# Attention scores from four half-height products a head, two heads side by side in 128 rows

## The chip, the cores and the metric

One Trainium2 chip, one core of it. The metric is the time of one execution in device microseconds; several runs are made and their median is taken. TensorE (PE) multiplies, VectorE (DVE) and ScalarE (ACT) work elementwise, GpSimd (POOL) does the same more slowly and issues some DMAs, SyncE (SP) issues most DMAs.

## The reference

Attention with a learned decay over 4 batches, 8 heads, 576 positions and 64 columns, then two mixture layers on the 2304 tokens. The change is in the attention alone:

```python
scores = scale * np.matmul(q, k.transpose(0, 1, 3, 2))
cum = np.cumsum(np.log(np.clip(f, 0.0001, 1.0)), axis=-1)
decay = cum[:, :, :, None] - cum[:, :, None, :]
scores = np.where(causal, -1000000000.0, scores + decay)
scores = scores - np.max(scores, axis=-1, keepdims=True)
attn = np.exp(scores)
attn = attn / (np.sum(attn, axis=-1, keepdims=True) + 1e-09)
return np.matmul(attn, v).astype(np.float32)
...
x = _moe_ref(x=x, **moe_kwargs)       # leaky relu between two matrices
return _moe2_ref(x=x, **moe2_kwargs)  # eight experts of fixed capacity
```

## The kernel before

The program has stages behind one another: attention (with the first products of the first mixture layer mixed in), the rest of that layer, the choice of experts, the experts. The change lies in the first, which ends with the last product av at 290.8 us of the profile.

Attention goes over 16 pairs of heads (`heads`), and each pair through three functions. `prepare` loads q and k, transposes them on TensorE into tile T, with both heads in 128 rows, and splits each number into a high part in float32r and the rest, the low part. `offsets` multiplies queries by keys with the queries in rows, finds each row's maximum on VectorE (into `nm`, tile `kept` holds the masked scores), sums the exponentials on ScalarE (into `sm`) and sends the maxima as rows back into the operands. `attend` makes the scores again, keys in rows, takes the exponential on ScalarE (P<-st), cuts at the diagonal on GpSimd, multiplies by v (av) and scales.

A score needs high x high, low x high, high x low and the added rows (running sum of the decay, maximum). Before, one head's operands fill the height of the array: `qa` has high over low parts, `ka` the high part twice, so qa x ka is one product of 128 rows; `qb` has the high part again and below it ones and maxima, `kb` the low part, running sums and ones, so qb x kb is the second, of 96 rows in `offsets` and of 128 in `attend` (lines 697, 698, 805 and 806). The second copies, in `ka`'s lower and `qb`'s upper half, are made by a DMA inside SBUF in every pair but the first (lines 643 and 645), and the first has extra ScalarE instructions instead (`again`, line 630). High and low parts are made a head at a time, in 64 rows (lines 602 to 615).

A block is a rectangle of queries and keys that are not all cut off: in `offsets` 64 and 192, 320, 448 and twice 288 keys for 128 queries, in `attend` 320, 448, 320 and 192, 256 and 64 queries for 128 keys. Each product goes into one PSUM bank of 128 x 512: tag `mx` with two banks for `offsets`, `st` with two for `attend`, one head at a time; T has two, av and h one each.

The order of work is set by `Plan.order`: each step is an `op` with an engine, an assumed duration, needs, a rank (12 a pair, plus places within it) and the buffers it takes and uses; a list scheduler lays the steps out, and they are issued in that order on each engine (`InOrder`). `mm_ns` (line 502) is the assumed duration of products: columns over 2.4 GHz, at least 107 ns, plus 3, a product; it has no term for a change between shapes of the array. All these steps have line 62 in the profile, so groups are told apart by tile. The early products h<-X,wh (line 904) and the preparation of weights (w, wbits, wsq, wst, wh) have ranks of their own and fill in.

av multiplies two heads in the two halves of the columns (64 each); T's last piece of each q and k has 64 rows.

Of the kernel before, what the change touches and what calls it, by code (L numbers as in the profile page):

```python
# [12 lines left out]
FT = mybir.dt.float32  # L13
FR = mybir.dt.float32r
# [3 lines left out]
OP = mybir.AluOpType  # L18
# [27 lines left out]
NK = 4  # L46
TB = 2
MX = 2
PBUF = 4
KH = "va"  # L50
# [147 lines left out]
def tile_kernel(ctx, tc, q, k, v, f, w_in, w_out, w_gate, w1, w2, out):  # L198
# [284 lines left out]
    with ExitStack() as c1:  # L483
# [13 lines left out]
        plan.depth = {"kept": NK, "h": 1, "T": TB, "mx": MX, "st": 2, "av": 1, "k": 3, "q": 3, "x3": 4, "vt": 2, "nm": 2, "sm": 2, "xh": 2, "xi": 2, "xr": 2,  # L497
                      "P": PBUF, "R": 2, "xt": 2, "w64": W64[0], "wsq": 1, "wbits": 2, "wst": 2, "w": WB, "wt": 1, "wq": 1, "ex": NE, "eg": NE}
        plan.chained = dict.fromkeys(("k", "q", "mx", "x3", "vt", "nm", "sm", "kept", "P", "av", "R", "xt", "ex", "eg"))
# [41 lines left out]
        QA, QB, KA, KB = zip(*([stp.tile([128, 2, W1], FR, name=f"{n}{i}") for n in ("qa", "qb", "ka", "kb")] for i in range(3)))  # L541
        pads = []
        for i in range(3):
            n = (i + 1) % 3
            pads.append([op("gp", ns, fn, (), 12 * n - 100) for ns, fn in (
                (1100, lambda i=i: gp.memset(QB[i][64:128].bitcast(FT), 0.0)),
                (1100, lambda i=i: gp.memset(KB[i][64:128].bitcast(FT), 0.0)),
                (1100, lambda i=i: gp.memset(QB[i][64:66].bitcast(FT), 1.0)),
                (1100, lambda i=i: gp.memset(KB[i][96:98].bitcast(FT), 1.0)),
                (142, lambda i=i: gp.memset(QA[i][:, :, :64].bitcast(FT), 0.0)),  # L550
                (142, lambda i=i: gp.memset(QB[i][:64, :, :64].bitcast(FT), 0.0)),
                (142, lambda i=i: gp.memset(KA[i][:, :, S:].bitcast(FT), 0.0)),
                (142, lambda i=i: gp.memset(KB[i][:64, :, S:].bitcast(FT), 0.0)))])

        def apart(x, *others):
            for y in others:
                if y is not None:
                    tc.declare_no_dep(x.ins, y.ins, reason="other columns")
# [4 lines left out]
        def prepare(n, own, z):  # L563
# [3 lines left out]
            qa, qb, ka, kb = (x[(n + 2) % 3] for x in (QA, QB, KA, KB))  # L567
# [18 lines left out]
            def part(j, t0, t1, z):  # L586
# [10 lines left out]
                def operands(u):  # L597
                    hi, lo = ((y[:, u, 64 + c0:64 + c1] for y in (qa[:64], qa[64:])) if j else
                              (y[:64, u, c0:c1] for y in (ka, kb)))
                    return mine[0][64 * u:64 * u + 64, :w], hi, lo  # L600

                def high(u):
                    x, hi, _ = operands(u)
                    if j:
                        act.mul(hi, x, 0.125)
                    else:
                        i = vec.tensor_copy(hi, x) if KH[u] == "v" else act.copy(hi, x)
                        apart(i, mine.get(("hi", 1 - u)), mine.get(("lo", 1 - u)))
                        mine["hi", u] = i

                def low(u):
                    x, hi, lo = operands(u)
                    i = vec.scalar_tensor_tensor(lo, x, 0.125 if j else 1.0, hi, op0=OP.mult, op1=OP.subtract)
                    apart(i, mine.get(("hi", 1 - u)))
                    mine["lo", u] = i
# [7 lines left out]
                for u in range(2):  # L623
                    e = "vec" if KH[u] == "v" and not j else "act"
                    a = op(e, (69 + 1.042 * w) if e == "vec" else 51 + .833 * w, lambda u=u: high(u), [o], z + ZH, (), [tb, sets[j]])
                    l = op("vec", 69 + 1.042 * w, lambda u=u: low(u), [a], z + ZL, (), [tb, sets[j]])
                    own["hi", j] = own.get(("hi", j), []) + [a]
                    outs[j] += [a, l]
                    if n == 0:
                        def again(u=u):  # L630
                            x = mine[0][64 * u:64 * u + 64, :w]
                            if j:
                                act.mul(qb[:64, u, 64 + c0:64 + c1], x, 0.125)
                            else:
                                act.copy(ka[64:, u, c0:c1], x)
                        outs[j].append(op("act", 51 + .833 * w, again, [o], z + ZH, (), [tb, sets[j]], plain=True))
            for j in range(2):
                part(j, 0, 3, z + 3 * j)
                part(j, 3, 5, z + 3 * j + 1)
            outs[0].append(op("sp", 450, lambda: sp.dma_start(kb[64:66, :, :S].bitcast(FT), cumd[:, H * b + h:H * b + h + 2]),  # L640
                              [outs[0][0]] + cums + (pads[(n + 2) % 3] if n < 3 else []), z + 1, (), [sets[0]], 30))
# [744 lines left out]
```

## Time and profile before

| | us |
|---|---|
| runs, median (lowest to highest) | 1017.56 (1015.96 to 1019.89) |
| profiled execution, its own time | 1021.9 |
| its span | 1020.2 |
| TensorE busy in the span | 967.6 |
| VectorE, ScalarE, GpSimd busy | 617.4, 458.0, 441.7 |
| last product av of attention starts | 290.8 |

The span runs from the first instruction to the last; the profiled execution's own time has 1.7 us around it. Busy times are of instructions as the profiler gives them; ends of products are modelled, so starts of neighbouring products tell more than their durations.

### The profile page before, as it was taken

How to read it: one execution, taken by the hardware profiler on the slowest of the kernel's cores; microseconds unless marked ns; L12 is line 12 of the kernel's file. 1: busy time of each engine (PE TensorE's matmuls, PEld its weight loads, DVE VectorE, ACT ScalarE, POOL GpSimd, SP SyncE). 2: the span in 40 equal slices, each digit the busy share in tenths (PEclk: the TensorE clock that was granted, in tenths of full speed). 3: DMA queues.
4: the chain of work that ended last, by engine and by line, in shares of the span. 5: the costliest groups of instructions: out<-in, count | busy, mean ns of one | idle time of the engine just before them, and what ended most of it. 6: DMA issues, size and time to landing. Idle time of an engine off the chain costs nothing.

```text
span 1020.2 us, 19998 instructions
## 1 busy us (share of the span) xinstructions
PE 967.6 (95%) x7171; PEld 811.4 (80%) x7171; DVE 617.4 (61%) x1687; ACT 458.0 (45%) x1181; POOL 441.7 (43%) x557
## 2 busy tenths in 40 slices
PE   5999999999989999999999999999996999999996
PEld 3666665877678899899987777777675999999996
DVE  6788897666537796862344465535745566666541
ACT  5798896766732232442232222212332455555531
POOL 6266776222358784820054444444674121222101
PEclk9999997999999999999989999999997999999998
DMA  5577786665479774553131212112143656666521
GB/s 114 132 192 195 196 225 170 161 171 137 116 250 357 252 235 154 176 162 87 43 118 60 62 63 62 42 63 63 63 115 116 202 171 191 211 192 198 163 74 36
DMA packets 145060, 147.65 MB, mean 145 GB/s; under 512 B 70048, under 2 KB 99232, under 8 KB 144704
## 3 DMA queue, kind: packets, MB, share of 16 engines
q1 hardware_dynamic: 141888, 136.93, 45.9%
q0 software_dynamic: 3072, 9.44, 3.2%
q8 instruction: 56, 0.92, 0.4%
q14 instruction: 44, 0.36, 0.1%
HBM read 106.67 MB, written 30.65 MB: 135 GB/s over the span
## 4 chain that ended last, share of the span: by engine, by line
PE 73%; issue 9%; DVE 5%; DMA 5%; POOL 4%; ACT 3%; SPq 0%; POOLq 0%; DVEq 0%; ACTq 0%
PE acc L1054 19%; PE h L62 18%; PE h L1110 6%; PE y L1123 6%; PE mx L62 5%; PE T L62 5%; PE av L62 5%; PE st L62 3%; DMA qb<-qa 3%; PE q_ct L1054 3%; POOL out L1131 1%; ACT qa L62 1%; POOL wsq L62 1%; ACT P L62 1%; ACT kept L62 1%
## 5 line engine op out<-in xcount | busy, mean ns | idle before, releaser
L62 PE MATMUL h<-X,wh 128*128 128x256 f32 x1728 | 231.2, 286 | 3.6 <-DVE g L62 2.6
L62 PEld LDWEIGHTS h<-X,wh 128*128 128x128 f32 x1728 | 213.6, 190 | 16.9 <-issue 9.3
L1054 PE MATMUL acc<-wh,gh 128*128 128x512 f32 x576 | 191.3, 406 | 0.0
L425 POOL TENSOR_TENSOR gl<-g,gh 128x512 fp32r<-128x512 f32 x72 | 96.4, 1340 | 113.2 <-ACT gh L424 102.0
L62 ACT ACTIVATE g<-h 128x256 f32<-128x256 f32 x144 | 55.3, 384 | 159.4 <-PE h L62 154.5
L1054 PEld LDWEIGHTS acc<-wh,gh 128*128 128x128 f32 x576 | 110.0, 192 | 20.9
L1054 PE MATMUL acc<-wh,gl 128*128 128x512 f32 x288 | 119.1, 413 | 0.0
L1110 PE MATMUL h<-XE,wh 128*128 128x288 f32 x768 | 118.7, 304 | 0.3 <-ACT XE L1101 0.3
L424 ACT CAST gh<-g 128x512 fp32r<-128x512 f32 x72 | 44.5, 621 | 163.4 <-PE acc L1054 133.3
L325 ACT CAST wh<-wst 128x512 fp32r<-128x512 f32 x132 | 80.0, 620 | 79.1 <-DMA wst<-in_moe_w 47.7
L62 DVE TENSOR_TENSOR wh<-wst,wh 128x512 fp32r<-128x512 f32 x132 | 90.7, 707 | 39.9 <-ACT wh L325 30.5
L1110 PEld LDWEIGHTS h<-XE,wh 128*128 128x128 f32 x768 | 106.9, 191 | 0.6 <-ACT XE L1101 0.6
L62 DVE TENSOR_TENSOR g<-g,h 128x256 f32<-128x256 f32 x144 | 59.9, 417 | 75.4 <-ACT g L62 74.7
L62 ACT ACTIVATE kept<-kept,nm 128x192 f32<-128x192 f32 (+2 forms) x192 | 97.7, 511 | 16.1 <-DVE nm L62 15.8
L1123 PE MATMUL y<-eh,wh 128*128 128x288 f32 x512 | 98.4, 296 | 0.2 <-issue 0.2
L1131 POOL DMA_INDIRECT out<-yo,ids x24 | 24.4, 1015 | 129.4 <-DVE yo L1130 120.1
L1123 PEld LDWEIGHTS y<-eh,wh 128*128 128x128 f32 x512 | 79.5, 188 | 0.5 <-issue 0.4
L62 DVE CUSTOM_DVE_ANT_0 kept<-mx,mask 128x192 f32<-128x192 f32 (+4 forms) x160 | 63.9, 426 | 25.2 <-PE mx L62 21.6
L62 PE MATMUL mx<-ka,qa 128*128 128x192 f32 (+2 forms) x192 | 69.5, 368 | 5.3 <-DVE nm L62 4.6
L62 PE MATMUL av<-P,vt 128*64 128x256 f32 (+4 forms) x512 | 71.2, 365 | 1.7 <-DVE R L62 1.4
L62 DVE SCALAR_TENSOR_TENSOR wbits<-w,wbits 128x256 int32<-128x256 int32 x128 | 70.2, 549 | 2.4
L62 ACT ACTIVATE P<-st 128x320 f32<-128x320 f32 (+2 forms) x128 | 62.8, 499 | 14.7 <-PE st L62 13.6
(187 smaller groups left out, 1681.7 us busy)
## 6 DMA issues: line engine op xcount, KB each, us to landing
wst<-in_moe_w SPq DMA_DIRECT2D x128, 256.0 KB
X<-xd SPq DMA_DIRECT2D x10, 1024.0 KB
gd<-g SPq DMA_DIRECT2D x36, 256.0 KB
g<-gd SPq DMA_DIRECT2D x36, 256.0 KB
w<-in_moe_w_in SPq DMA_DIRECT2D x32, 256.0 KB
w<-in_moe_w_out SPq DMA_DIRECT2D x32, 256.0 KB
xd<-xt SPq DMA_DIRECT2D x16, 320.0 KB
R<-invd SPq DMA_DIRECT2D x32, 144.0 KB
```

The source lines that it names most:

```text
L62: r = getattr(self.engine, name)(*a, **k)
L325: A.copy(r[u][0], x)
L424: A.copy(gh, g)
L425: G.tensor_tensor(gl, g, gh, op=OP.subtract)
L1054: tc.keep_in_program_order(PE.matmul(*a, **k))
L1110: PE.matmul(h[:, :CAP], w, X[:, c, x, :], start=n == 0, stop=n == 3 * NC - 1)
L1123: PE.matmul(yt[c][:, :CAP], w[:, s], a, start=j == 0 and n == 0, stop=j == NJ - 1 and n == 2)
L1131: sd = G.indirect_dma_start(out=out[:, :], out_offset=bass.IndirectOffsetOnAxis(ap=ids[:, 3 * e + t:3 * e + t + 1], axis=0), in_=y, in_off ...
```

## The change

Six operands a set take the place of four, each of 128 rows with the pair's first head in the upper and its second in the lower 64: `qh`, `ql` (high and low part of the queries), `kh`, `kl` (of the keys) and `qr`, `kr` (ones, maxima, running sums and zeros). High and low parts are made for both heads in one instruction of 128 rows, and all high parts on ScalarE. The copies by DMA and `again` are gone. Running sums and maxima go into `kr` and `qr` with one DMA a head, so two of each in place of one.

A score is now four products a head: high x high, low x high, high x low, and the added rows. The two heads alternate, each in its half of the rows. In `offsets` the fourth product has 32 rows, all others have 64. Both heads' products go into one PSUM buffer `s` of two banks, one bank a head; there are two such buffers, for `offsets` and `attend` together, in place of mx and st. The exponential of P is one instruction for both heads.

```diff
-        plan.depth = {"kept": NK, "h": 1, "T": TB, "mx": MX, "st": 2, "av": 1, ...
+        plan.depth = {"kept": NK, "h": 1, "T": TB, "s": 2, "av": 1, ...
...
-        QA, QB, KA, KB = zip(*([stp.tile([128, 2, W1], FR, name=f"{n}{i}") for n in ("qa", "qb", "ka", "kb")] for i in range(3)))
+        QH, QL, QR, KH, KL, KR = zip(*([stp.tile([128, W1], FR, name=f"{n}{i}") for n in ("qh", "ql", "qr", "kh", "kl", "kr")] for i in range(3)))
...
-                for u in range(2):
-                    e = "vec" if KH[u] == "v" and not j else "act"
-                    a = op(e, (69 + 1.042 * w) if e == "vec" else 51 + .833 * w, lambda u=u: high(u), [o], z + ZH, (), [tb, sets[j]])
-                    l = op("vec", 69 + 1.042 * w, lambda u=u: low(u), [a], z + ZL, (), [tb, sets[j]])
...
+                a = op("act", 51 + .833 * w, high, [o], z + ZH, (), [tb, sets[j]])
+                outs[j] += [a, op("vec", 69 + 1.042 * w, low, [a], z + ZL, (), [tb, sets[j]])]
...
-            if n:
-                outs[0].append(op("sp", 625, lambda: sp.dma_start(ka[64:, :, :S].bitcast(FT), ka[:64, :, :S].bitcast(FT)),
-                                  own["hi", 0], z + 3, (), [sets[0]], 820))
-                outs[1].append(op("sp", 625, lambda: sp.dma_start(qb[:64, :, 64:].bitcast(FT), qa[:64, :, 64:].bitcast(FT)),
-                                  own["hi", 1], z + 6, (), [sets[1]], 820))
...
-                    sc[0] = p = ps.tile([128, 512], FT, name="mx", tag="mx", bufs=plan.depth["mx"])
+                    sc[0] = p = ps.tile([128, 2, 512], FT, name="s", tag="s", bufs=2)
                     for t, i, c0, c1, a in ts:
-                        o = p[:, a:a + c1 - c0]
-                        kl, ql = slice(c0, c1), slice(128 * t, 128 * t + 128)
-                        pe.matmul(o, qa[:, u, ql], ka[:, u, kl], start=True, stop=False)
-                        pe.matmul(o, qb[:96, u, ql], kb[:96, u, kl], start=False, stop=True)
+                        for m, (x, y, r) in enumerate(((qh, kh, 64), (ql, kh, 64), (qh, kl, 64), (qr, kr, 32))):
+                            for u in range(2):
+                                d = slice(64 * u, 64 * u + r)
+                                pe.matmul(p[:, u, a:a + c1 - c0], x[d, 128 * t:128 * t + 128], y[d, c0:c1], start=m == 0, stop=m == 3)
...
+                        for m, (x, y) in enumerate(((kh, qh), (kl, qh), (kh, ql), (kr, qr))):
+                            for u in range(2):
+                                d = slice(64 * u, 64 * u + 64)
+                                pe.matmul(p[:, u, col[n]:col[n + 1]], x[d, 128 * i:128 * i + 128], y[d, 64 + f0:64 + f1], start=m == 0, stop=m == 3)
...
-                def weights(u, sc):
-                    act.activation(own["P", name][:, u, :col[-1]], sc[0][:, :col[-1]], AF.Exp)
+                def weights():
+                    act.activation(own["P", name][:, :, :col[-1]], sc[0][:, :, :col[-1]], AF.Exp)
```

TensorE's queue before, within one pair late in the stage (st: scores of one head; mx: offsets of the next pair; out<-moving, stationary operand):

```order
L62 MATMUL av<-P,vt 64x64 x2
L62 MATMUL st<-qa_132,ka_134 128x448
L62 MATMUL st<-qb_133,kb_135 128x448
L62 MATMUL mx<-ka_138,qa_136 128x320
L62 MATMUL mx<-kb_139,qb_137 128x320
L62 MATMUL T<-ident,x_1665 128x128
L62 MATMUL T<-ident,x_1665 128x64
L62 MATMUL st<-qa_132,ka_134 128x320
L62 MATMUL st<-qb_133,kb_135 128x320
L62 MATMUL mx<-ka_138,qa_136 128x448
L62 MATMUL mx<-kb_139,qb_137 128x448
L62 MATMUL h<-X,wh 128x256 x3
```

And now, at the like place (s<-qh,kh and its kind: scores; s<-kh,qh and its kind: offsets; x2 is one product a head):

```order
L60 MATMUL av<-P,vt 64x64 x2
L60 MATMUL s<-qh_138,kh_141 128x320 x2
L60 MATMUL s<-qh_138,kl_142 128x320 x2
L60 MATMUL s<-ql_139,kh_141 128x320 x2
L60 MATMUL s<-qr_140,kr_143 128x320 x2
L60 MATMUL s<-kh_147,qh_144 128x288 x2
L60 MATMUL s<-kh_147,ql_145 128x288 x2
L60 MATMUL s<-kl_148,qh_144 128x288 x2
L60 MATMUL s<-kr_149,qr_146 128x288 x2
L60 MATMUL T<-ident,x_1301 128x128
L60 MATMUL T<-ident,x_1301 128x64
L60 MATMUL h<-X,wh 128x256 x6
```

Where before only av and the last piece of T left the full shape, now every group of scores or offsets stands in another one, and the last product of an offset (kr, qr) in a third.

SP's queue before, over the same part of a pair (R: the inverse sums; vt: v; X: operands of the early products):

```order
L62 DMA X<-xd_63 128x2x256
L62 DMA R<-invd 64x576
L62 DMA xd_64<-xt 128x2x320
L62 DMA ka_138<-ka_138 64x2x576
L62 DMA R<-invd 64x576
L62 DMA qb_137<-qa_136 64x2x576
L62 DMA vt<-in_v 128x4x64 x2
```

And now:

```order
L60 DMA qr_134<-xr 2x5x128 x2
L60 DMA kr_149<-cumd 2x576 x2
L60 DMA X<-xd_63 128x2x256 x2
L60 DMA invd<-xi 12x128
L60 DMA x_2189<-in_k 128x4x64 x2
L60 DMA vt<-in_v 128x4x64 x2
L60 DMA xd_64<-xt 128x2x320
L60 DMA R<-invd 64x576 x2
```

The two copies ka<-ka and qb<-qa are gone, and xr and the running sums go out in two pieces each.

## Rows read from the trace of the kernel before

**Rows 1.** The chain that ended last, by line, 11 to 291 us.
```profile
by line: PE mx L62 18.7%; PE av L62 18.1%; PE st L62 12.3%; DMA qb<-qa 10.8%; PE h L62 9.5%; PE T L62 8.8%; ACT qa L62 3.4%; issue 3.2%; ACT P L62 3.0%; ACT kept L62 3.0%; DVE kept L62 1.6%; DMA x<-in_k 1.3%; DVE qa L62 1.1%; DMA w<-in_moe_
```

**Rows 2.** Windows: busy us of PE, PEld, DVE, ACT, POOL; TensorE clock, DMA share, GB/s.
```profile
60.00:150.00 90.00, 85.37 (x549) 57.85 (x548) 79.76 (x276) 77.77 (x244) 64.51 (x93) 1.00 0.78 200
196.00:255.00 59.00, 59.00 (x423) 46.82 (x420) 38.27 (x135) 40.67 (x133) 15.82 (x27) 1.00 0.60 157
```

**Rows 3.** TensorE instructions on tile T, 59 to 152 us (duration ns, first and last start).
```profile
...
L62 PE MATMUL T<-ident,sm x7: 269/274/276, 59.8 to 151.6; 128*12 128x128 f32 x7
...
```

**Rows 4.** The same, 190 to 256 us.
```profile
...
L62 PE MATMUL T<-ident,sm x4: 275/275/275, 195.5 to 254.6; 128*12 128x128 f32 x4
...
```

**Rows 5.** TensorE instructions on tile h, 195.5 to 254.6 us.
```profile
...
L62 PE MATMUL h<-X,wh x144: 277/282/388, 197.1 to 253.9; 128*128 128x256 f32 x144
...
```

**Rows 6.** TensorE in order of time, 290.9 us on (start us, us, instruction).
```profile
...
290.99 7.46 PE L62 MATMUL h<-X,wh 128*128 128x256 f32 x60
```

**Rows 7.** The same, 104 us on: products at full height and width.
```profile
104.70 0.31 PE L62 MATMUL mx<-kb,qb 96*128 96x320 f32 x1
104.84 0.37 PE L62 MATMUL mx<-ka,qa 128*128 128x448 f32 x1
105.05 0.37 PE L62 MATMUL mx<-kb,qb 96*128 96x448 f32 x1
105.25 0.27 PE L62 MATMUL T<-ident,x 128*128 128x128 f32 x1
```

**Rows 8.** The same, 102 us on: values between two scores.
```profile
102.30 0.28 PE L62 MATMUL st<-qb,kb 128*128 128x64 f32 x1
102.51 0.55 PE L62 MATMUL av<-P,vt 128*64 128x192 f32 x4
102.98 0.36 PE L62 MATMUL mx<-ka,qa 128*128 128x192 f32 x1
103.18 0.28 PE L62 MATMUL mx<-kb,qb 96*128 96x192 f32 x1
```

**Rows 9.** The same, 128 us on: two transposes, the second of 64 rows.
```profile
128.53 0.47 PE L62 MATMUL T<-ident,x 128*128 128x128 f32 x2
128.93 0.41 PE L62 MATMUL st<-qa,ka 128*128 128x320 f32 x1
129.19 0.30 PE L62 MATMUL st<-qb,kb 128*128 128x320 f32 x1
129.33 0.37 PE L62 MATMUL mx<-ka,qa 128*128 128x448 f32 x1
```

**Rows 10.** TensorE weight loads in order of time, 103 us on.
```profile
103.20 0.19 PEld L62 LDWEIGHTS mx<-ka,qa 128*128 128x128 f32 x1
103.32 0.19 PEld L62 LDWEIGHTS mx<-kb,qb 96*128 96x128 f32 x1
```

**Rows 11.** ScalarE by line and form, 28 to 300 us (busy us, mean ns of one, idle before).
```profile
...
L62 ACT ACTIVATE P<-st 128x320 f32<-128x320 f32 x64 | 27.8, 434 | 11.7 <-PE st L62 11.0
...
L62 ACT ACTIVATE P<-st 128x512 f32<-128x512 f32 x32 | 18.9, 592 | 1.8 <-PE st L62 1.8
...
```

**Rows 12.** VectorE, the same columns and stretch.
```profile
...
L62 DVE SCALAR_TENSOR_TENSOR qa<-T,qa 64x384 fp32r<-64x384 f32 x28 | 15.6, 556 | 2.2 <-ACT qa L62 1.3
...
L62 DVE CUSTOM_DVE_ANT_0 kept<-mx,mask 128x320 f32<-128x320 f32 x30 | 14.6, 486 | 5.7 <-PE mx L62 5.4
...
L62 DVE CAST ka<-T 64x384 fp32r<-64x384 f32 x13 | 7.0, 541 | 0.1
...
```

**Rows 13.** What TensorE waited for, 11 to 300 us (total us, times, longest).
```profile
...
PE mx L62 <- DMA qb<-qa: 2.9, 6, 0.8
...
```

**Rows 14.** Windows around a fall of the clock, columns as in rows 2.
```profile
160.00:165.00 5.00, 4.01 (x24) 2.63 (x24) 4.92 (x17) 4.65 (x17) 2.58 (x5) 1.00 1.10 225
165.00:170.00 5.00, 3.98 (x25) 2.70 (x25) 3.13 (x13) 3.13 (x11) 3.24 (x6) 0.79 0.85 161
170.00:175.00 5.00, 5.00 (x20) 2.40 (x16) 2.24 (x8) 2.19 (x7) 3.45 (x4) 0.50 0.60 173
```

More of the change, by code (lines that the diff above doesn't have):

```diff
@@ L47 @@
 TB = 2
-MX = 2
 PBUF = 4
-KH = "va"
 ZG = 60
@@ L544, in tile_kernel @@
             n = (i + 1) % 3
[L545 to L558, printed above, removed]
+            fs = [(560, lambda i=i: gp.memset(QR[i].bitcast(FT), 0.0)), (560, lambda i=i: gp.memset(KR[i].bitcast(FT), 0.0))]
+            for u in range(2):
+                fs += [(560, lambda i=i, u=u: gp.memset(QR[i][64 * u:64 * u + 2].bitcast(FT), 1.0)),
+                       (560, lambda i=i, u=u: gp.memset(KR[i][64 * u + 32:64 * u + 34].bitcast(FT), 1.0))]
+            for x, c in ((QH, 0), (QL, 0), (KH, S), (KL, S)):
+                fs.append((100, lambda x=x[i], c=c: gp.memset(x[:, c:c + 64].bitcast(FT), 0.0)))
+            pads.append([op("gp", ns, fn, (), 12 * n - 100) for ns, fn in fs])
         heads = [(b, hp) for b in range(B) for hp in range(H // 2)]
@@ L595, in flip, with high, low @@
                         pe.transpose(p[:, 128 * t - c0:128 * t - c0 + m], x3[j][:m, t].rearrange("p s d -> p (s d)"), ident[:m, :m])
[L597 to L603, printed above, removed]
+                hi, lo = (y[:, 64 + c0:64 + c1] for y in (qh, ql)) if j else (y[:, c0:c1] for y in (kh, kl))
+                def high():
                     if j:
-                        act.mul(hi, x, 0.125)
+                        act.mul(hi, mine[0][:, :w], 0.125)
                     else:
[L607 to L615, printed above, removed]
+                        act.copy(hi, mine[0][:, :w])
+                def low():
+                    vec.scalar_tensor_tensor(lo, mine[0][:, :w], 0.125 if j else 1.0, hi, op0=OP.mult, op1=OP.subtract)
                 first = j not in sets
@@ L684, in offsets, with part @@
             mins, tots = [], []
-            def part(u, ts, z, last):
+            def part(ts, z, last):
                 sc = {}
@@ L721, in part @@
                 nb, sb = own["nmb"]
-                ms = []
-                hold = []
-                for x in ts:
-                    m = op("vec", 85 + 1.042 * (x[3] - x[2]), lambda x=x: maximum(*x), [o] + last[:1], z + 1, ["kept"] if not hold else (), [mxb, nb] + hold)
-                    hold = hold or m.got
-                    ms.append(m)
-                mins.extend(ms)
-                if ts[0][0] == 4:
-                    if ts[0][1] == 0:
-                        return (o, ms[0], hold[0], total)
-                    last.append(ms[0])
@@ L733, in part @@
[L733 to L745 removed]
+                r = []
@@ new lines, in part @@
+                for u in range(2):
+                    ms, hold = [], []
+                    for x in ts:
+                        m = op("vec", 85 + 1.042 * (x[3] - x[2]), lambda u=u, x=x: maximum(u, *x), [o] + [y[0] for y in last[u:u + 1]], z + 1, ["kept"] if not hold else (), [sb0, nb] + hold)
+                        hold = hold or m.got
+                        ms.append(m)
+                    mins.extend(ms)
+                    r.append((ms[0], hold[0], lambda u=u: total(u, *ts[0])))
+                    if ts[0][0] == 4 and ts[0][1] == 0:
+                        continue
+                    for x, m in zip(ts, ms):
+                        tots.append(op("act", 280 + .833 * (x[3] - x[2]), lambda u=u, x=x: total(u, *x), [m], z + 2, (), hold + [nb, sb]))
+                    if last:
+                        tots.append(op("act", 280 + .833 * 288, last[u][2], [ms[0]], z + 2, (), [last[u][1], nb, sb]))
@@ L813, in causal @@
                     gp.affine_select(x, x, pattern=[[0, 2], [1, w]], base=0, channel_multiplier=-1, compare_op=OP.is_ge, fill=0.0)
[L814 to L820 removed]
+                o = op("pe", 2 * mm_ns(*(y - x for _, x, y in blocks)), product, own["max"], z, ["s", "P"], kq)
+                pb = o.got[1]
+                acts = [op("act", 51 + 1.666 * col[-1], weights, [o], z + 1, (), [o.got[0], pb])]
                 for n, (i, f0, f1) in enumerate(blocks):
```

91 lines of the change are left out of this document (32 added, 59 removed).

## The prediction

> **What bounds the kernel now.** I read the attention stage alone, the first 291 us, since the change touches nothing behind it. The chain of waits comes first: in the stage it runs mainly over TensorE's products (mx 18.7%, av 18.1%, st 12.3%, h 9.5%, T 8.8%), and the one foreign piece is the copy qb<-qa with 10.8%, some 30 us, which the change removes [rows 1]. A chain shows what stood last before each step, not what would stand there next. So I look at how full the engines are: from 60 to 150 us TensorE is busy 85 of 90 us, VectorE 80, ScalarE 78; from 196 to 255 us TensorE never rests and the other two are at 38 and 41 of 59 us [rows 2]. The first stretch is close to a tie, the second is TensorE's alone.
>
> The length of one head pair turns this into numbers. One transpose T<-ident,sm stands in every pair. Between the first and the last of seven lie 91.8 us, so an early pair takes 91.8 / 6 = 15.3 us [rows 3]. Late, four of them span 59.1 us, or 19.7 us a pair [rows 4]; in that time TensorE also did 144 products of the first MoE layer [rows 5], at 7.46 / 60 = 0.12 us each [rows 6], 17.6 us in all with the unrounded 0.122. Without them a late pair is (59.1 - 17.6) / 3 = **13.8 us of pure TensorE work**. An early pair thus holds at most 15.3 - 13.8 = 1.5 us that faster VectorE, ScalarE or DMA could give back. The direct sign agrees: in the whole stage TensorE stood idle for qb<-qa for only 2.9 us in 6 places [rows 13]; the other 27 us of the chain's copy ran beside earlier products.
>
> **The change, part by part.** *The copies and the half-height pieces.* Two copies in SBUF a pair disappear (15 pairs; the first had extra ScalarE instructions instead, which go too), and one more row transfer each for kr and qr appears; SP issues fewer in all. On VectorE the low parts, eight instructions a pair, become four: 0.556 us for each of the wide ones removed, and the cast of k (0.541 us wide) goes to ScalarE [rows 12]. With the narrow ones that is about 2.7 us less of some 13.6 a pair. On ScalarE the exponentials of P cover both heads at once. From 0.434 us at 320 columns to 0.592 at 512 is 0.82 ns a column and 0.17 us fixed [rows 11]; four fixed parts go, 0.7 us a pair, and the high parts save about as much. All of this lies beside TensorE's 13.8 us. I count it only as the cover of the 1.5 us: I let every early wait vanish, which is generous. If TensorE got shorter, it would be worth more; it doesn't.
>
> *The streams.* Before, a block has two products a head, four for both heads, one after the other at full height. Now there are eight of half height, in four steps of two heads side by side. If the two run together, the steps are as many as before: twelve blocks a pair times four is 48. A step of full height lasts 0.14 us at 320 columns and 0.20 at 448 [rows 7], which is columns over 2.4 GHz plus about 0.01 us; narrow ones are held by the weight loads, 0.11 to 0.12 us apart [rows 10]. No row shows two row halves together. The nearest is av, whose two heads lie in the two column halves: four instructions of 192 columns take 0.47 us from start to the next product [rows 8]; one after the other, with two passes each, they would need 8 x 192 / 2.4 GHz = 0.64 us, together 0.32. So halves do run together, and I take that. The step's own overhead may grow: from nothing to the 0.05 us a step that av's surplus leaves when a change of shape is taken out. I take 0.01 us, near the low end, since av's surplus is for two passes and fresh weights; 48 x 0.01 = **0.5 us a pair**, bounds 0 and 2.4.
>
> *The changes of shape.* This is the term that decides. Products that use the array at full height, in halves of 64 rows, of 32 rows or of 64 columns alternate on TensorE's queue. Counted in the built order up to the last av product, the shape changes 283 times before and **471 times** now: into 64 rows 32 becomes 143, into 32 rows 0 becomes 96 (the offsets' fourth product uses 32 rows a head), into full shape 136 becomes 123, into 64 columns 115 becomes 109. (T's 20- and 12-column transposes count as full.) The price comes from two places. Around a 64-row transpose: from 128.53 to 129.33 us lie two transposes and two 320-column scores, 0.80 us [rows 9]; at the usual steps, 0.11 + 0.11 + 0.145 + 0.145, it would be 0.51. That is 0.29 us for the way in and out, 0.145 a change. Around an av pair: 102.30 to 103.18 is 0.88 us [rows 8]; 0.11 + 0.32 + 0.11 would be 0.54, so 0.34, 0.17 a change. In both, part of it is spent before the new shape starts and part in the first step after (0.26 us for 320 columns in place of 0.145 [rows 9]): the weights of the new shape aren't loaded ahead. I take 0.16 us: 188 / 16 = 11.75 more changes a pair, times 0.16, is **1.9 us a pair**. The upper bound is 0.17. The lower one: whether 64 to 32 rows counts as a change, no row shows. If those 96 cost nothing, 92 remain at 0.145, 0.8 us a pair. I take them at the full price, since both kinds of change seen cost nearly the same.
>
> [...]
>
> *Shared banks.* Scores and offsets had two banks each, one head a bank; now both share two pairs of banks. An offset pair is free only after both heads' maxima, 2 x 0.486 us at 320 columns [rows 12]. A product pair comes every 16.2 / 12 = 1.35 us and there are two, so about 2.7 us are there for a product of 0.6 to 0.9 us and a read of 1 us: enough, if VectorE isn't late by more than 0.8 us. I cost it at nothing; its failure is a rival.
>
> **The sum.** A pair becomes 13.8 + 1.9 + 0.5 = 16.2 us. Nine early pairs: 16.2 - 15.3 = +0.9 each, +8 us. The other seven (four with MoE products, the first and the last ones): +2.4 each, +17 us. Together **+25 us**. The profiled execution took 1021.9 us, of which 1020.2 us are its span, so it would become 1047; it lies 4.3 us over the median of 1017.6, against which I predict 1043 us. A measurement of this kernel can tell about 0.5% from no change, 5 us.
>
> **The rivals.** *The height change is free and the cover pays* (no change). With 92 changes at 0.145 us and no step overhead a pair needs 14.6 us: 9 x -0.7 early, 7 x +0.8 late, about 0: 1017 us. For it: no row shows a change from 64 to 32 rows. Against: two other changes cost alike. Chance 0.11.
>
> *Faster.* A change costs less than 0.07 us, because most of the 188 fall where TensorE would have waited anyway: the copy is in the chain with 30 us [rows 1], and the first step after a wait has its weights loaded late already. Then 188 x 0.07 = 13 us only equals the early waits of 9 x 1.5 = 13.5 us, and below it the change wins; with changes that cost nothing it is 1017.6 - 13.5 = 1004 us. Against: late pairs have no waits [rows 2]. Chance 0.08.
>
> *The halves don't overlap.* If the weights of the two heads are loaded one after the other, a step lasts at least 2 x 0.11 = 0.22 us. The twelve blocks' steps sum to 1.65 us at one product each, 6.6 us a pair; at 0.22 they are 10.6: +4 us a pair, +64 us, 1107 us; with products one after the other 6.6 a pair, 1149. For it: no row with row halves. Against: the av rows [rows 8]. Chance 0.09.
>
> In this kernel weights are loaded while earlier products at the same rows still run: loads stand 0.11 to 0.12 us apart at full height [rows 10]. [...]
>
> *A wait or the clock.* The shared banks make TensorE wait 0.2 us at each of twelve products a pair: +38 us on top, 1081 us. Or the granted clock falls more often: it fell from 1.00 to 0.50 after a stretch in which TensorE was idle 1 us of 5 [rows 14], and each 5 us at 0.50, the 1.2 GHz level, loses 2.5 us; ten more such windows cost 25 us, 1068 us. Changes of shape thin out the streams. Chance 0.14.
>
> **How the numbers follow.** The forecast has 0.58; its own range is 1030 to 1058, from 0.145 us a change without step overhead to 0.17 us with three times mine. Slower by over 0.5%: 0.58 + 0.09 + 0.14 = 0.81; no change 0.11; faster 0.08. The range leaves out the faster case and the one without overlap, and reaches from the no-change case to the wait and clock: 1015 to 1080 us.
>
> **What would show it.** Right: an early pair of about 16 us, a late one of about 22 with its MoE products, TensorE without idle time, the two heads' products starting almost together, the first step after 64 to 32 rows about 0.1 us longer than usual, VectorE and ScalarE with more idle time. Wrong: the two heads' products a whole step apart (halves don't overlap); late pairs still at 19.7 us (changes are free); idle TensorE before s products that ends with a maximum or an exponential (banks); the end of the stage before 291 us.

## The result, and the profile after

The changed kernel takes **1028.66 us** (median of five runs, 1027.47 to 1030.21), against 1017.56 before; the ratio is 1.011, with a 95% interval of 1.008 to 1.0139. It is slower, by 11 us, where 25 were forecast. The two profiled executions have spans of 1026.9 and 1020.2 us, 6.7 apart, since that of before lay 4.3 us over its median. The last av product starts at 298.2 us instead of 290.8, so the loss lies in attention, as expected, and nothing behind it changed by more than a microsecond.

The chain of waits, 11 to 298 us, answers to [rows 1]:

```profile
by line: PE s L60 47.4%; PE av L60 17.5%; PE h L60 11.4%; PE T L60 10.7%; ACT kept L60 2.8%; issue 2.2%; ACT P L60 1.8%; DVE kept L60 1.4%; POOL xt L60 1.2%; DMA vt<-in_v 1.1%; DVE R L60 0.6%; DMA kr<-cumd 0.6%; DVE wbits L60 0.4%; DVE kl L
```

The copy's 10.8% are gone, and what took their place is TensorE itself: s, av, h and T together 87%, where mx, st, av, h and T had 67%. The windows, columns as in [rows 2]:

```profile
60.00:150.00 90.00, 89.50 (x839) 60.53 (x839) 67.47 (x246) 69.53 (x210) 65.43 (x95) 1.00 0.63 172
196.00:255.00 59.00, 59.00 (x490) 41.80 (x490) 25.49 (x105) 33.74 (x102) 14.37 (x25) 1.00 0.37 106
```

In the early stretch TensorE now rests 0.5 us of 90 instead of 4.6, and VectorE has 12 and ScalarE 8 us less to do. The relief came, and so did the load. What TensorE waited for, 11 to 305 us (total us, times, longest), answers to [rows 13]:

```profile
PE av L60 <- DVE R L60: 1.8, 2, 1.1
PE s L60 <- DMA kr<-cumd: 1.4, 1, 1.4
PE T L60 <- PE T L60: 1.0, 1, 1.0
PE s L60 <- ACT P L60: 0.6, 2, 0.3
```

No line there waits for a maximum, and the exponentials hold back 0.6 us in all: the shared banks hold nothing up. The length of a pair, by the transposes on T as in [rows 3, 4], 59 to 152 and 165 to 257 us:

```profile
L60 PE MATMUL T<-ident,sm x7: 275/275/276, 60.8 to 151.9; 128*12 128x128 f32 x7
...
L60 PE MATMUL T<-ident,sm x5: 274/275/275, 166.7 to 256.1; 128*12 128x128 f32 x5
```

An early pair takes (151.9 - 60.8) / 6 = 15.2 us, against 15.3 before: no loss at all, where 16.2 were forecast. In the late stretch lie 159 products h:

```profile
L60 PE MATMUL h<-X,wh x159: 274/282/389, 172.2 to 255.3; 128*128 128x256 f32 x159
```

Less 159 x 0.122 = 19.4 us a late pair takes (89.4 - 19.4) / 4 = 17.5 us, against 13.8 before: +3.7, where +2.4 were forecast. So the loss sits in the late pairs: at the ninth transpose on sm the two traces are 0.3 us apart (151.9 and 151.6 us), at the last av 7.4. The +3.7 holds for these four pairs; from the ninth transpose to the last av, seven pairs, it is +7.0 in all, since the kernel before loses some 5 us more there to a fall of the clock [rows 14] and the products h lie otherwise over the pairs.

The changes of shape can be watched at one offset product. TensorE in order of time, 120.4 us on (start us, us, instruction; x2 is one product a head):

```profile
120.24 0.34 PE L60 MATMUL av<-P,vt 128*64 128x64 f32 x4
120.50 0.41 PE L60 MATMUL s<-kh,qh 64*128 64x320 f32 x2
120.76 0.31 PE L60 MATMUL s<-kh,ql 64*128 64x320 f32 x2
120.90 0.31 PE L60 MATMUL s<-kl,qh 64*128 64x320 f32 x2
121.14 0.41 PE L60 MATMUL s<-kr,qr 32*128 32x320 f32 x2
121.48 0.28 PE L60 MATMUL T<-ident,sm 128*12 128x128 f32 x1
121.69 1.08 PE L60 MATMUL av<-P,vt 128*64 128x256 f32 x8
```

and its weight loads, same columns (in brackets the idle time before):

```profile
120.50 0.19 PEld L60 LDWEIGHTS s<-kh,qh 64*128 64x128 f32 x2
120.61 0.19 PEld L60 LDWEIGHTS s<-kh,ql 64*128 64x128 f32 x2
120.76 0.18 PEld L60 LDWEIGHTS s<-kl,qh 64*128 64x128 f32 x2
121.14 0.18 PEld L60 LDWEIGHTS s<-kr,qr 32*128 32x128 f32 x2 [0.19 <-issue]
```

The pair of 320-column products takes 0.14 us at its plain step (120.76 to 120.90), as one product of full height did [rows 7]: the two heads do run together. The first step in the shape takes 0.26. The step before the 32-row product takes 0.24, the 32-row product itself 0.34, the T behind it 0.21. The weights ql and kl are loaded while the product before runs; those of the 32 rows are not, their load waits until 121.14. So a change costs about 0.1 us at the end of the old shape and 0.1 us in the first step of the new one, and 64 to 32 rows is a change like the others.

**An account of TensorE.** To put all of it in numbers I went through the starts of TensorE's products up to the last av, in every profile, and split each distance from one start to the next: columns over 2.4 GHz plus 0.006 us, at least 0.11 us for a weight load (twice that in the stretches of half clock); 0.09 us where the shape changes behind it; 0.105 us (0.05 for 64 columns) where it is the first in its shape; the rest is waiting. The first 38 us count as half clock in both kernels: the clock's records begin there, and until then a step of 448 columns takes 0.37 us, later 0.20. The constants are fitted to steps like those above, so the split is an estimate, good to a few microseconds a column. Changes are counted as executed.

| us, to the last av | before | after |
|---|---|---|
| changes of shape (number) | 46.5 (282) | 80.1 (468) |
| waits | 34.9 | 11.1 |
| lost to half clock | 15.8 | 12.7 |
| score products | 102.2 | 102.8 |
| T, av and h | 86.3 | 86.3 |

The differences are +33.6, -23.8, -3.1, +0.6 and 0; their sum, +7.3, is the 7.4 us by which the stage grew. The waits are what the other terms leave over. The profile's own lists of waits have less, 20.1 us before and 5.7 after from 11 us on, and the price of a change moves the two together: at 0.15 us, which rows64 below gives for most of the stage, changes are +28 and waits -18. In the early pairs nine more changes (26 against 17) took the place of the 1.9 us that the account has as waits of a pair before; in late ones full of products h there are some twenty more (40 and 44 against 20) and there was nothing to fill.

### The profile page after: what moved, and what is told of

Read it like the earlier page. It is cut to its first block, busy times and chain, and to the rows that moved or that the text cites. A ratio compares the mean times of both kernels' runs of the same rounds, so it can differ in the third digit from the quotient of the medians.

```text
span 1026.9 us, 21248 instructions
## 1 busy us (share of the span) xinstructions
PE 986.9 (96%) x7939; PEld 816.0 (79%) x7939; DVE 574.2 (56%) x1591; ACT 433.9 (42%) x1077; POOL 438.3 (43%) x563
## 4 chain that ended last, share of the span: by engine, by line
PE 78%; issue 9%; DVE 5%; POOL 3%; DMA 3%; ACT 2%; SPq 0%; POOLq 0%; ACTq 0%; DVEq 0%
PE h L60 19%; PE acc L1012 19%; PE s L60 13%; PE h L1068 6%; PE y L1081 6%; PE T L60 6%; PE av L60 5%; PE q_ct L1012 3%; POOL out L1089 1%; DMA X<-xd 1%; ACT kept L60 1%; PE T L1058 1%; DVE wbits L60 1%; DVE wh L60 1%; PE T L1086 1%
## 5 line engine op out<-in xcount | busy, mean ns | idle before, releaser
L422 ACT CAST gh<-g 128x512 fp32r<-128x512 f32 x72 | 44.5, 621 | 162.4 <-PE acc L1012 131.7
L60 DVE CUSTOM_DVE_ANT_0 kept<-s,mask 128x192 f32<-128x192 f32 (+4 forms) x160 | 61.6, 427 | 54.6 <-PE s L60 54.0
L60 PE MATMUL av<-P,vt 128*64 128x256 f32 (+4 forms) x512 | 68.5, 358 | 2.2 <-DVE R L60 1.8
L1081 PE MATMUL y<-el,wh 128*128 128x288 f32 x256 | 67.7, 296 | 0.0
L60 POOL TENSOR_SCALAR_AFFINE_SELECT P<-P 128x256 f32<-128x256 f32 (+1 forms) x80 | 29.5, 386 | 85.0 <-ACT P L60 84.9
```

What stands on the lines that cost most here:

```text
L60: r = getattr(self.engine, name)(*a, **k)
L422: A.copy(gh, g)
L1081: PE.matmul(yt[c][:, :CAP], w[:, s], a, start=j == 0 and n == 0, stop=j == NJ - 1 and n == 2)
```

## The experiments

The theory that they test, A in the expectations, is this account: changes of shape cost about 0.18 us each, the one from 64 to 32 rows included, and the relief of the other engines gives back waits alone. The rivals: that the height change is free; that something else in the change (banks, pieces, copies) sets the time; that a change of shape costs nothing where TensorE would have waited.

**rows64: the fourth offset product in 64 rows.** A constant stationary tile `q1` (ones in the two rows of running sums of each head, zeros in the others) lets the fourth product use 64 rows like the other three. The 96 changes into 32 rows go; what follows saves some more, 468 to 351.

```diff
+        Q1 = stp.tile([128, 128], FR, name="q1")
...
-                        for m, (x, y, r) in enumerate(((qh, kh, 64), (ql, kh, 64), (qh, kl, 64), (qr, kr, 32))):
+                        for m, (x, y) in enumerate(((qh, kh), (ql, kh), (qh, kl), (Q1, kr))):
                             for u in range(2):
-                                d = slice(64 * u, 64 * u + r)
+                                d = slice(64 * u, 64 * u + 64)
+                                w = x[d] if m == 3 else x[d, 128 * t:128 * t + 128]
```

> The changed kernel with one edit: the offsets' fourth product has 64 rows a head instead of 32, with a constant stationary operand (ones in two rows, zeros elsewhere), so the result stays the same. Changes of shape on TensorE's queue up to the last av product: 468 become 351, 117 fewer. Theory A (changes of shape are what the change costs, about 0.18 us each, and TensorE has hardly any waits left): 117 x 0.18 = 21 us less, some of it given back as waits, so 1007 to 1014 us, and an early pair of 13.5 to 14 us in place of 14.8. Theory B (the loss comes from the shared banks or other waits, changes from 64 to 32 rows are free): within 4 us of 1028.7. Theory C (the clock): no change of the pair's length, only the falls move.

Measured: **1005.25 us** (1003.03 to 1006.37), 0.987 of before (0.9823 to 0.9918). The same four products in its trace, in order of time:

```profile
108.07 0.31 PE L60 MATMUL s<-kh,ql 64*128 64x320 f32 x2
108.22 0.31 PE L60 MATMUL s<-kl,qh 64*128 64x320 f32 x2
108.36 0.31 PE L60 MATMUL s<-kr,q 64*128 64x320 f32 x2
108.60 0.27 PE L60 MATMUL T<-ident,sm 128*12 128x128 f32 x1
```

The step ahead of the fourth product is 0.14 instead of 0.24 us, the fourth's own 0.24 instead of 0.34. With 117 changes fewer it is 23.4 us faster than the kernel after, 0.20 us a change, and 2 us under the expected range. The stage is 22.6 us shorter; 8.3 of them lie ahead of the second transpose on sm (37.7 us, 46.0 in the kernel after), with 22 changes fewer. There the clock rose sooner too: its records begin with 1.00 at 18.2 us here and at 38.0 us in the kernel after. TensorE 30 us on, first here, then in the kernel after:

```profile
29.93 0.37 PE L60 MATMUL s<-qh,kl 64*128 64x448 f32 x2
30.13 0.37 PE L60 MATMUL s<-ql,kh 64*128 64x448 f32 x2
```

```profile
30.20 0.57 PE L60 MATMUL s<-kh,ql 64*128 64x448 f32 x2
30.58 0.57 PE L60 MATMUL s<-kl,qh 64*128 64x448 f32 x2
```

A step of 448 columns takes 0.20 us in the one and 0.38 in the other. Behind the second transpose 95 changes fewer are 14.3 us, 0.15 a change. By the account 21.3 of the 22.6 us are changes; the half clock is some 3 us less and waits 1 more. Why the clock rose sooner no run shows. The height change is not free, and this one term decided the sign of the whole change: without it the kernel is faster than before.

**pieces: the old half-height pieces.** The exponentials of P and the high and low parts a head at a time again, the rest as after.

```diff
-                a = op("act", 51 + .833 * w, high, [o], z + ZH, (), [tb, sets[j]])
-                outs[j] += [a, op("vec", 69 + 1.042 * w, low, [a], z + ZL, (), [tb, sets[j]])]
+                for u in range(2):
+                    e = "vec" if u == 0 and not j else "act"
+                    a = op(e, (69 + 1.042 * w) if e == "vec" else 51 + .833 * w, lambda u=u: high(u), [o], z + ZH, (), [tb, sets[j]])
+                    outs[j] += [a, op("vec", 69 + 1.042 * w, lambda u=u: low(u), [a], z + ZL, (), [tb, sets[j]])]
...
-                acts = [op("act", 51 + 1.666 * col[-1], weights, [o], z + 1, (), [o.got[0], pb])]
+                acts = [op("act", 51 + .833 * col[-1], lambda u=u: weights(u), [o], z + 1, (), [o.got[0], pb]) for u in range(2)]
```

> The changed kernel with the half-height pieces back: high and low parts a head at a time in 64 rows (eight low parts on VectorE, k's high part of one head on VectorE), and P's exponential a head at a time on ScalarE; operands, products and banks stay as changed. It tells what took the early waits away. Theory A1 (the copies by DMA did, and TensorE's longer pair of 14.8 us covers VectorE's 13.6 us): 1027 to 1034 us. Theory A2 (the relief of VectorE and ScalarE did): the early waits of nearly 2 us a pair come back, 9 x 1.9 = 17 us, 1040 to 1047 us.

Measured: **1056.48 us** (1050.71 to 1068.04), 1.0415 of before (1.0339 to 1.0491), some 27 us over the kernel after. The relief was worth more than the waits it took away. What TensorE waited for, 11 to 325 us, and windows around two falls of the clock (columns as in [rows 2]):

```profile
PE s L60 <- ACT P L60: 4.5, 7, 1.1
```

```profile
85.00:97.60 12.60, 11.68 (x117) 8.13 (x115) 10.83 (x33) 9.85 (x29) 7.53 (x12) 1.00 0.61 157
97.70:114.70 17.00, 17.00 (x84) 9.96 (x80) 12.02 (x39) 9.37 (x29) 9.46 (x11) 0.50 0.40 114
152.30:169.30 17.00, 17.00 (x84) 9.97 (x80) 10.43 (x40) 8.36 (x27) 6.93 (x10) 0.50 0.37 97
```

By the account the loss to half clock grew by 15.6 of the 22.3 us by which this execution's stage is longer, and waits by some 6: twice the granted clock stood at 0.50 for 17 us (at 0.50 a step of 448 columns takes 0.37 us in the kernel after, from 276.06 to 276.43, against 0.20 at 1.00). The first of these two falls came after a stretch in which TensorE had been idle 0.9 us of 12.6, as the one before the change came after idle time [rows 14]; each lost 8.5 us, far more than that idle time.

**pieceP and pieceH: one half of it each.** The exponentials of P alone a head at a time (the last two lines of the diff above), and the high and low parts alone (the lines above them).

> The changed kernel with one part of the run of the pieces: P's exponential a head at a time on ScalarE, everything else as changed. ScalarE gets four fixed parts a pair back, 0.7 us. If that relief mattered: half or more of the pieces' 28 us, 1040 us or more. If VectorE's pieces did: 1026 to 1036 us.

> The changed kernel with the other part: high and low parts a head at a time in 64 rows (2.7 us a pair more on VectorE, 0.8 on ScalarE), P's exponential for both heads at once. If VectorE's relief took the early waits away: 1040 to 1056 us. If ScalarE's P did: 1026 to 1036 us.

Measured: **1030.95 us** (1027.88 to 1037.51), ratio 1.0127 (1.0051 to 1.0203), and **1059.05 us** (1053.24 to 1061.6), ratio 1.0403 (1.0335 to 1.0471). The high and low parts carry the loss, 30 us over the kernel after; the joint exponential brought 2 us, which its runs don't tell from nothing. pieceH, what TensorE waited for, and its early window:

```profile
PE s L60 <- ACT P L60: 5.0, 9, 1.0
```

```profile
60.00:150.00 90.00, 87.86 (x679) 57.94 (x677) 67.52 (x220) 61.24 (x179) 54.04 (x74) 0.79 0.47 132
```

TensorE waits for exponentials here although these are the joint ones of the kernel after; that the pieces ahead of them on ScalarE hold them up is likely, and not tried by itself. The mean clock of the window is 0.79; the account has 30.3 us at half clock against 12.7.

**copies: the two copies by DMA back.** They fill extra tiles `qc` and `kc`, which two of the four products read in place of qh and kh.

```diff
+                outs[0].append(op("sp", 625, lambda: sp.dma_start(own["kc"][:, :S].bitcast(FT), kh[:, :S].bitcast(FT)), own["hi", 0], z + 3, (), [sets[0]], 820))
+                outs[1].append(op("sp", 625, lambda: sp.dma_start(own["qc"][:, 64:].bitcast(FT), qh[:, 64:].bitcast(FT)), own["hi", 1], z + 6, (), [sets[1]], 820))
...
-                        for m, (x, y, r) in enumerate(((qh, kh, 64), (ql, kh, 64), (qh, kl, 64), (qr, kr, 32))):
+                        for m, (x, y, r) in enumerate(((qh, kh, 64), (ql, own["kc"], 64), (own["qc"], kl, 64), (qr, kr, 32))):
```

> The changed kernel with the two copies by DMA back in every pair but the first: the high parts are copied inside SBUF (288 KB each, as before), and two of the four products read the copies, so they wait for them as before; the half-height pieces stay away. Together with the run of the pieces it tells which part of the change took the waits away. Theory A1 (the copies were the wait, as the chain of before had it with 10.8%): the early waits of nearly 2 us a pair come back, 9 x 1.9 = 17 us, 1040 us or more. Theory A2 (the relief of VectorE and ScalarE did it, the copies ran beside earlier products): 1023 to 1034 us, early pairs under 15.3 us.

Measured: **1049.44 us** (1043.41 to 1057.84), 1.0271 of before (1.0197 to 1.0346), 21 us over the kernel after by the medians, 16 by the two ratios to before. The time says that taking the copies away was worth that much; how, the trace shows in part. TensorE on tile T, 60 to 139 us, and windows:

```profile
L60 PE MATMUL T<-ident,sm x5: 275/275/276, 63.2 to 123.8; 128*12 128x128 f32 x5
```

```profile
130.00:139.00 9.00, 7.72 (x78) 5.38 (x76) 7.15 (x21) 6.61 (x17) 8.68 (x12) 1.00 0.94 254
139.12:183.49 44.37, 44.37 (x222) 27.03 (x224) 19.30 (x73) 18.88 (x57) 19.17 (x28) 0.50 0.40 120
```

An early pair takes (123.8 - 63.2) / 4 = 15.2 us, as without the copies. Then TensorE is idle 1.3 us of nine, with the DMA engines 94% busy, and the clock stands at 0.50 for 44 us, though TensorE never rests in them. This stretch and one of 13.7 us from 207.4 us on make most of the 24 us that the account has at half clock above the kernel after (36.7 against 12.7). That the copies made the idle time is likely; what made the clock fall, and stay down so long, no run shows. The profiled execution, 1057.84 us, is the longest of the four, so the others lost less in this way.

**noalt: one head's four products, then the other's.** The same products with the two loops exchanged, in `offsets` (shown) and in `attend`.

```diff
-                        for m, (x, y, r) in enumerate(((qh, kh, 64), (ql, kh, 64), (qh, kl, 64), (qr, kr, 32))):
-                            for u in range(2):
+                        for u in range(2):
+                            for m, (x, y, r) in enumerate(((qh, kh, 64), (ql, kh, 64), (qh, kl, 64), (qr, kr, 32))):
```

> The changed kernel with the two heads' products no longer alternating: all four of one head, then all four of the other, in the same shapes. It tells what the overlap of the row halves is worth. If a product runs beside the one before it only when that is in the other half, a block takes seven steps instead of four: 102.8 x 3/4 = 77 us more, about 1105 us. If TensorE overlaps the halves whatever the order: 1028 us. If they hardly overlapped before: 1028 us too, but the steps of the changed kernel speak against it.

Measured in a single run: **1288.53 us**, far over what was expected. TensorE in order of time in `offsets`, 504 us on, at full clock:

```profile
504.06 0.47 PE L60 MATMUL s<-kh,qh 64*128 64x448 f32 x1
504.37 0.36 PE L60 MATMUL s<-kh,ql 64*128 64x448 f32 x1
504.57 0.36 PE L60 MATMUL s<-kl,qh 64*128 64x448 f32 x1
504.86 0.47 PE L60 MATMUL s<-kr,qr 32*128 32x448 f32 x1
```

One head's 448-column product takes the 0.20 us alone (504.37 to 504.57) that a pair takes in alternation. In `attend` the exchange did no such thing: in all 96 of its blocks the second head's first product starts before the first head's last one, and in none of the 96 blocks of `offsets`. In order of time in `attend`, 60 us on, behind a product av:

```profile
60.47 0.48 PE L60 MATMUL s<-qh,kl 64*128 64x320 f32 x2
60.74 0.48 PE L60 MATMUL s<-ql,kh 64*128 64x320 f32 x2
```

A pair takes 0.27 us there, as one 320-column product does at half clock (0.27 us in the kernel before, 178.11 to 178.38, at 0.50). All eight products of an `attend` block have 64 rows; in `offsets` the first head's product of 32 rows now stands in the queue between the two heads. That this change of shape keeps the heads apart is likely; `offsets` in 64 rows and in this order was not run.

By the account score products rise from 102.8 to 170.2 us and changes from 80.1 to 116.1, since each head now enters 32 rows by itself. The larger part is the clock, 168.8 us against 12.7. Windows of its trace:

```profile
66.80:100.00 33.20, 33.20 (x135) 21.64 (x135) 10.13 (x41) 11.76 (x34) 9.10 (x14) 0.50 0.26 71
100.00:165.80 65.80, 65.80 (x261) 43.15 (x263) 20.41 (x82) 22.70 (x67) 19.97 (x28) 0.50 0.27 71
```

TensorE never rests in these 99 us, and the clock stays at 0.50. Nor did it rest in the 27 us ahead; of these the clock stood at 1.00 for the last 3.4 alone, where its records begin (63.4 us), and the steps at 60 us still have the length of half clock. So in `offsets` the gain of halves that run together hangs on the order in which they are issued, in `attend` it does not.

**bmerge: fewer changes in the kernel before.** All av products of a half behind one another, 282 changes to 121.

```diff
-            for i in range(3):
-                values(0, i, z + 5 + (i > 0))
+            values(0, range(3), z + 6)
...
-            for i in range(5):
-                values(1, i, z + 8 + (i > 1))
+            values(1, range(5), z + 9)
```

> The kernel before with the products av of a half of the queries made in one go (three, then five blocks) instead of block by block; the result stays the same. Changes of shape: 282 become 121. Theory A (a change costs TensorE time in the kernel before too, 0.16 us each): 161 x 0.16 = 26 us less where TensorE is the bound, and some of it back as waits, since av now waits for the last P: 992 to 1008 us. Rival (before, changes fall mostly into waits; a longer av group only makes P and its buffers late): 1015 us or more.

Measured: **1025.86 us** (ten runs, 1017.34 to 1027.77), 1.0062 of before (1.003 to 1.0093): no gain, a small loss. What TensorE waited for, 11 to 300 us:

```profile
PE mx L62 <- DVE nm L62: 8.5, 19, 1.7
PE T L62 <- DVE kb L62: 5.5, 7, 1.6
PE T L62 <- DVE xh L62: 5.2, 7, 1.2
...
PE st L62 <- ACT P L62: 4.4, 10, 0.9
```

Changes fall from 46.5 to 22.2 us and waits rise from 34.9 to 57.5. av in pieces was what TensorE did while it waited for the maxima. The time fits the rival, that a change of shape which fills a wait is free; but merged products av also wait for the last P of their half, and the run does not part the two.

**r64h, r64hmerge, r64h_o20, r64ht: better versions.** All from rows64. r64h issues the early products h twelve at a time instead of three; r64hmerge also has av merged as in bmerge; r64h_o20 lets the planner charge 180 ns a change and prefer the same shape within 20 ranks; r64ht cuts each transposition into four and one blocks instead of three and two, which keeps the 64-row transposes by themselves.

```diff
-                for c in range(NC):
-                    o = op("pe", 355, lambda c=c, f=product: f(c), [loads[c], o] + wi0[c]["ops"], ...
+                o = op("pe", 355 * NC, lambda f=product: [f(c) for c in range(NC)], loads + sum(...
...
-                part(j, 0, 3, z + 3 * j)
-                part(j, 3, 5, z + 3 * j + 1)
+                part(j, 0, 4, z + 3 * j)
+                part(j, 4, 5, z + 3 * j + 1)
```

> The kernel with 64 rows throughout (the run of that edit), and the early products h made twelve at a time (all four parts of a value) instead of three. Changes of shape: 351 become 312, all of them in the late pairs. If changes are the price there too: 39 x 0.18 = 7 us less than the 64-row kernel's 1005, 995 to 1002 us. If longer h groups only make other products late: 1005 us or more.

> As the run before, and the products av of a half of the queries in one go, the edit that brought nothing in the kernel before: there 24 us of changes went and 23 us of waits came. Changes of shape: 312 become 190. If the waits there came from VectorE and ScalarE, which have less to do now, most of 122 x 0.18 = 22 us stays: 975 to 990 us. If they come from the longer way of P and av themselves, the waits eat it again: 995 to 1010 us.

> As the run with h twelve at a time, and the list scheduler reckons 180 ns for each change of shape and prefers a ready product of the shape just used, up to 20 ranks. Changes of shape: 312 become 287. If only their number counts: 25 x 0.18 = 4 us less than that run, 991 to 998 us. If the preference upsets the order of the pairs: more than that run.

> The kernel with 64 rows throughout and h twelve at a time, and the transposes of q and k cut into four of 128 rows and one of 64, instead of three and two, so that the 64-row transpose can stand beside products of 64 rows. Changes of shape: 312 become 269. If changes still are the price: 43 x 0.18 = 8 us less than that kernel's 1000.5, 990 to 997 us. If the longer first transposes make high and low parts late: 1000 us or more.

| | changes | us for them | waits | half clock | median us | ratio to before (95%) |
|---|---|---|---|---|---|---|
| rows64 | 351 | 58.8 | 12 | 10 | 1005.25 | 0.987 (0.9823 to 0.9918) |
| r64h | 312 | 51.0 | 15 | 10 | 1000.49 | 0.9806 (0.9737 to 0.9874) |
| r64hmerge | 190 | 33.7 | 33 | 12 | 1003.78 | 0.985 (0.9778 to 0.9922) |
| r64h_o20 | 287 | 47.1 | 17 | 17 | 1005.45 | 0.9839 (0.9767 to 0.9911) |
| r64ht | 269 | 44.5 | 16 | 11 | 998.44 | 0.9796 (0.9735 to 0.9857) |

The three middle columns are the account's, in us to the last av, the waits and the half clock to a few microseconds: the clock's records begin at 15.7 to 20.6 us in these five, not at 38. r64hmerge saves 17.3 us of changes against r64h and pays some 18 in waits, most of them on exponentials (11 to 300 us):

```profile
PE s L60 <- ACT P L60: 13.8, 20, 1.1
```

r64h_o20 saves 3.9 and pays some 2 in waits and 8 at half clock. r64ht is the fastest run of all, 30 us under the kernel after; its interval doesn't tell it from r64h. Both beat both kernels.

## Why the prediction was right in sign, and wrong in size

**What bounds the kernel, and the sign.** Right: TensorE was bound, the copy in the chain was cover and not bound, and the changes of shape made the kernel slower. The size was wrong: +11.1 us where +25 was forecast. 1028.66 lies in the wide range, 1015 to 1080, but 14 us under the number and just under the forecast's own range, 1030 to 1058. The steps that failed are two terms of the sum: the overhead of a step, taken as 0.5 us a pair and measured as 0, and the waits that the change gives back, taken as 13.5 us and by the account 18 to 24.

**Changes of shape, 188 x 0.16 = +30 us.** Right in mechanism and about right in size: +33.6 us by the account, 0.18 us each, or +28 at the 0.15 that rows64 gives behind the stage's beginning. The choice to count the 96 changes from 64 to 32 rows in full was right, and rows64 shows it, at 0.15 to 0.20 us a change. What was wrong is where they fall: spread as 11.75 a pair, they are nine more in an early pair and some twenty more in a late one full of products h.

**"The step's own overhead may grow ... 0.5 us a pair".** This step failed: it is 0. Two halves of 320 columns take 0.14 us a step, of 448 columns 0.20, as the full height did. Score products cost +0.6 us in the whole stage instead of 7.7. The sum av's surplus was read from holds two passes (in the kernel before 0.16 us a step of 192 columns behind the first, twice 192 over 2.4 GHz) and fresh weights, as the text said; it was no row for this.

**"An early pair thus holds at most 1.5 us".** This step failed too, and with it the sum's count of nine early pairs alone. The bound took the late pair as pure work, but a late pair has more changes of shape in it than an early one (20 against 17), because products h stand between, so 13.8 us was not what an early pair needs. Waits were 1.9 us in an early pair by the account, and the stage's beginning, which the sum took as a late pair without waits, had more: before the first T<-ident,sm they fell from 10.9 to 4.4 us (in the profile's own lists, behind the first load of k, from 9.2 to 3.6). In all 23.8 us of waits went instead of 13.5. With the step above this makes 10.3 + 7.1 us; less 3.6 for the changes and plus 3.1 of half clock, 17 of the 18 us between the forecast +25 and the stage's +7.4. At 0.15 us a change the waits that went are 18 us, and the miss in them 5. So the overhead's 7 us are sure, and the waits' share is 5 to 10.

**Copies, pieces and banks at nothing, beyond the waits.** The banks: right, nothing waits for a maximum. The pieces and copies: in the sum they stand for the waits that vanished, and the text took their relief as small; put back one at a time they cost 30 and 21 us, and by the account most of that at half clock, which the text had named only as a rival. The kernel after had one fall in the stage, 3.4 us at 273.5 us, that before one of 13.7 us at 167.9, which lost 6.8 us; more falls, the rival "a wait or the clock", is what the runs without the relief show.

**The rivals.** *No change* fails on the price of 64 to 32 rows. *Faster* had a true piece: in early pairs the changes fell where TensorE had waited, which cancels them there; in late pairs it didn't. *Halves without overlap* fails in the changed kernel, where the two heads start 10 ns apart or less in 676 of 768 pairs of products and run together in all blocks, and comes true in noalt's `offsets` alone. With halves, too, weights are loaded while products of the same rows run: the loads at 120.61 and 120.76 stand 0.15 and 0.14 us ahead of their own products, beside the ones before in the same halves, as at full height [rows 10].

**What would show it.** Late pairs of 22 us with their MoE products: 89.4 / 4 = 22.4, right. TensorE without idle time, the heads together, 0.1 us at 64 to 32 rows: right. Early pairs of 16: wrong, 15.2. The stage's end after 291 us: right.

## What to carry to other kernels

Count changes of the array's shape in the issued order and price each at the 0.15 to 0.2 us measured here; then ask of each whether TensorE would have waited there: where it would, taking the changes out gained nothing (bmerge, r64hmerge). If one product of a group stands in another shape than the rest, pad it to theirs, as rows64 does with a constant tile: 23 us of 1029. And before a stage without waits is taken as the pure work of one with waits, compare what else lies in the two.

## What was not expected of the hardware

- Two halves of the array need not be issued alternately to run at once. In noalt's `attend` the second head's products ran beside the first's in all 96 blocks, although each stands four places behind it in the queue; in `offsets`, with a product of 32 rows between the heads, they did in none. In order of time, at a granted clock of 0.50 (a pair of 448 columns takes 0.37 us there, from 122.45 to 122.82):

```profile
121.80 0.37 PE L60 MATMUL T<-ident,x 64*128 64x64 f32 x1
121.93 0.78 PE L60 MATMUL s<-qh,kh 64*128 64x448 f32 x2
122.45 0.63 PE L60 MATMUL s<-qh,kl 64*128 64x448 f32 x2
122.82 0.63 PE L60 MATMUL s<-ql,kh 64*128 64x448 f32 x2
```

- The granted clock can stand at 0.50 with TensorE busy throughout: 44 us in copies, 99 us in noalt. A fall followed idle time in some cases (in the 10 us ahead of it 2.1 us before, 0.9 in pieces and pieceH, 1.3 in copies) and came with next to none in others (0.2 us ahead of the one after, 0.1 in pieceP, 0.0 in noalt, where the clock had stood at 1.00 for 3.4 us). So idle time doesn't tell alone whether it falls, and what does stays open.
